# Cosine attention and a Highway layer on one core: the casts of v, the engines of the small operations, and the order of the Highway sum

## The chip, the cores and the metric

The kernel runs on one core of a Trainium2 chip. A core has a matrix engine (PE, with its weight loads as PEld), a vector engine (DVE), a scalar engine (ACT), GpSimd (POOL) and a synchronising engine (SP) that issues most DMAs here. Each engine runs its own instructions in program order; semaphores order them against each other. Matmuls write to PSUM[...]; DVE and ACT read it. The metric is the device time in microseconds of one execution, the median over the runs.

## The reference

Attention over 8 batches of 12 heads, 448 positions, head dimension 64, with q and k normalised, and then a Highway layer over the 3,584 x 768 result:

```python
q_n = q / (norm(q) + 1e-06);  k_n = k / (norm(k) + 1e-06)
attn = softmax(q_n @ k_n.T / tau)          # tau = 0.1
x = (attn @ v)                             # heads side by side: 3584 x 768
H = maximum(x @ w_h, 0.0)
T = 1.0 / (1.0 + exp(-(x @ w_t + b_t)))
out = T * H + (1.0 - T) * x
```

## The kernel before

**Tiling.** The heads are taken four at a time: 24 "quads" Q, three to a batch. A quad is loaded as two tiles raw (q and k, 128 partitions x 14 groups of 64); a batch's v is loaded in three pieces into vr. Each position is p x 7 + c, so a partition holds seven positions of a head.

**Steps of a quad.** `squares` makes sq = raw x raw on the engine that SQ_E names for the quad (ACT in one instruction, POOL in two, lines 369 and 373) and sums it on DVE (line 389); where FOLDS is 1 or 2, POOL first folds the row once or twice (lines 416 and 422). `rsqrt` takes one over the root: on ACT with Ln and Exp for the first seven quads, later on DVE with a shift and two Newton steps over a batch. `norms` multiplies (line 525, the engine from NORM: one instruction on DVE, two on POOL), and qn is turned by PE and a copy or by a DMA transpose on SP (TURN). `cast_v` casts v from 32 to 16 bits into vm (line 583) by the table VM: "A" is ACT, "D" is DVE with both sides read in order, "U" is DVE with the two inner dimensions exchanged on both sides, so that its reads are 64 elements apart. vm has a 65th column of 2.0, so that attention times vm gives the sum of the row too.

**Scores and products.** `quad` makes the scores in seven pieces (line 620, PSUM tiles sp, two of them), ACT takes the exp (line 631), PE multiplies with vm (line 671, tile u), and DVE divides (lines 704, 722, 714). Because of the 2.0, what is kept in x is half of the attention's output.

**The FFN.** 28 tiles n of 128 rows: three for each batch and one more for each two batches (xtail). x is turned by PE with a copy (DVE or ACT) or by DMA (table XT), then four quarters follow: w_t and w_h for the first 384 columns, w_t and w_h for the last. A quarter accumulates 6 matmuls, or 7 where the bias enters as a row of ones, in one of two PSUM tiles pt. In the last six tiles (TAIL) it is the two halves of a score tile sp, and DVE adds the bias (line 836). With t = tanh of the w_t quarter (line 846) and h the w_h quarter, three DVE operations make the sum:

```python
g  = (t - 1) * x           # line 850, tt and x both in SBUF
pt = (t + 1) * h           # line 867, in place in PSUM
o  = max(pt, 0) - g        # line 874
```

**The order.** No loop writes the instructions in the order in which they run. `Plan.run` lists every operation with an engine, a guessed duration, what it depends on and a due time, and simulates: on each engine it takes the ready operation with the smallest start plus LATE times its due time. An operation marked "lock" is taken to exclude POOL while it runs. Where the durations or tables change, the order on all engines, SP's DMA queue among them, changes with them. `P.buf(name, n)` makes the owner of a buffer wait for all users of the one n before it.

Of the kernel before, what the change touches and what calls it, by code (L numbers as in the profile page):

```python
# [8 lines left out]
FP32 = mybir.dt.float32  # L9
FP16 = mybir.dt.float16  # L10
# [10 lines left out]
class Plan:  # L21
# [6 lines left out]
    SLACK = 1.3  # L28
    AHEAD = 15
    NEAR = 60  # L30
    LATE = 0.04

    def __init__(self):
        self.ops = []
# [128 lines left out]
def kernel(  # L163
# [11 lines left out]
    nc = tc.nc  # L175
# [42 lines left out]
    ones_row = const.tile([128, 128], FP16)  # L218
    eps = const.tile([128, 1], FP32)
    NV = 2  # L220
    SQ_E = ("DPPAAAAAAAAAAAAAAPPPPAAP", "PPAPPPPPPPAAAAAAAAPAPPAA")
    FOLDS = "000000000002012200000210"
    NORM = ("DPPPPDPPPPDPPPPPPPDPDDDP", "DDDPPPPPPPPDPPPPPPPPPPPP")
    TURN = ("ADDDSSSSSSSSSSSSSSSSSSSS", "DDDDASSSSSSSSSSSSSSSSSSS")
    XT = "DDDDDDSDSAASSSSSAASSSSSSDAAA"
    ENG = {"A": "ACT", "D": "DVE", "P": "POOL"}
    PAIR = 12
    NEWT = 8
    LATER = 3
    W_AT = 16  # L230
    RS = "AAAAAAADDDDDDDDDDDDDDDDD"
    VM = "UAAAAAUUUUUUUDDDDDDADDAU"
    TAIL = 6
    vm_b = [const.tile([128, 6, C, 66], FP16, name=f"vm{i}") for i in range(NV)]
    e_b = [const.tile([128, 14 * S + 64], FP16, name=f"e{i}") for i in range(2)]
# [170 lines left out]
    def folds(Q, t, sq_ops, level, ring):  # L406

        ringf, waitf = P.buf(f"fold{t}", 2)
        first = []
        for i in range(1):  # L410
            def f(i=i):
                if i == 0:
                    st["fold", Q, t] = fold_p.tile([128, NT, D // 2], FP32, name=f"fold{t}")
                g = slice(0, NT)
                sq = st["sq", Q, t]
                nc.gpsimd.tensor_add(  # L416
                    st["fold", Q, t][:, g, :], sq[:, g, 0 : D // 2], sq[:, g, D // 2 : D]
                )
            first.append(op("POOL", 900, None, sq_ops + ([("first", first)] if first else waitf), f))
        def h():  # L420
            x = st["fold", Q, t]
            nc.gpsimd.tensor_add(
                x[:, :, 0 : D // 4], x[:, :, 0 : D // 4], x[:, :, D // 4 : D // 2]
            )
        last = op("POOL", 520, None, first, h) if level == 2 else first[0]
        ring += first
        ringf += first + [last] * (level == 2)
        st["ring_fold", Q, t] = ringf
        return [last]

    logs = []

    def rsqrt_act(b, qd, reds):

# [13 lines left out]
    def rsqrt(b, qd, n, reds):  # L448
        due = None
        if RS[NQ * b + qd] == "A":  # L450
            return rsqrt_act(b, qd, reds)
        eng = "DVE" if b < NEWT else "POOL"
        lens = (90 if n == 1 else 150, 190 if n == 1 else 290)

        def tiles():
            n2, rs = nrm_tiles(b)
            return n2[:, qd : qd + n, :], rs[:, qd : qd + n, :]

        def f0():
            x, y = tiles()  # L460
            nc.vector.tensor_single_scalar(
                y.bitcast(I32), x.bitcast(I32), 1, ALU.arith_shift_right
            )

        def f1():
            _, y = tiles()
            nc.vector.tensor_scalar(
                out=y.bitcast(I32), in0=y.bitcast(I32), scalar1=-1.0,
                scalar2=float(0x5F3759DF), op0=ALU.mult, op1=ALU.add,
            )  # L470

        ring_ta, wait_ta = P.buf("ta", 2)
        last = op("DVE", lens[0], due, reds + wait_ta, f0, kind="lock")
        last = op("DVE", lens[0], due, [last], f1, kind="lock")
        ta = {}

        def newton(i, it):
            e = nc.vector if eng == "DVE" else nc.gpsimd

            def f():  # L480
                x, y = tiles()
                if i == 0 and it == 0:
                    ta[0] = ta_p.tile([128, NQ, NG], FP32, name="ta")
                a = ta[0][:, 0:n, :]
                if eng == "DVE":
                    if i == 0:
                        e.scalar_tensor_tensor(out=a, in0=y, scalar=-0.5, in1=x, op0=ALU.mult, op1=ALU.mult)
                    elif i == 1:
                        e.tensor_mul(a, a, y)
                    else:  # L490
                        e.scalar_tensor_tensor(out=y, in0=a, scalar=1.5, in1=y, op0=ALU.add, op1=ALU.mult)  # L491
                elif i == 0:
                    e.tensor_mul(a, y, x)
                elif i == 1:
                    e.tensor_mul(a, a, y)
                elif i == 2:
                    e.tensor_scalar(out=a, in0=a, scalar1=-0.5, scalar2=1.5, op0=ALU.mult, op1=ALU.add)
                else:
                    e.tensor_mul(y, a, y)
            return f  # L500

        for it in range(2):
            for i in range(3 if eng == "DVE" else 4):
                last = op(eng, lens[0] if eng == "DVE" else lens[1], due, [last], newton(i, it),
                          kind="lock" if eng == "DVE" else "")
                ring_ta.append(last)
        return last
# [67 lines left out]
    def cast_v(b):  # L575
        ring, wait = P.buf("vm", NV)
        vm = vm_b[b % NV]
        outs = []
        for i in range(NQ):
            def f(i=i):  # L580
                how = VM[NQ * b + i]
                dims = "p i d c" if how == "U" else "p i c d"
                (nc.scalar.copy if how == "A" else nc.vector.tensor_copy)(  # L583
                    vm[:, 2 * i : 2 * i + 2, :, 0:D].rearrange(f"p i c d -> {dims}"),
                    st["vr", b][:, 2 * i : 2 * i + 2, :].rearrange(f"p i (c d) -> {dims}", c=C),
                )
            how = VM[NQ * b + i]
            outs.append(op(
                "ACT" if how == "A" else "DVE", {"A": 840, "D": 540, "U": 990}[how], None,
                wait + [o_fv[b % NV], st["gotv", b][i]], f, kind="lock" if how == "D" else "",  # L590
            ))
        ring += outs
        st["ring_vr", b] += outs
        st["vm", b] = (ring, outs)


# [2 lines left out]
    def quad(Q):  # L599
# [78 lines left out]
        for rnd, when in enumerate((t_step(Q, 6), t_step(Q, 6) + 2.5)):  # L678
# [3 lines left out]
            for i in range((6, 2)[rnd]):  # L682
                def f(i=i, rnd=rnd, key=key):
                    if i == 0:
                        st[key] = u_ps.tile([128, 2, 512], FP32, name="u")
                    t, h = divmod(i, 2)
                    av(st[key], i, h, 384 - 64 * par if rnd else 128 * t)
                a = op("PE", 220, when + 0.01 * i,
                       list(exps.values()) + [o_vm[qd], o_fv[Q % 2]] + ([("first", ops)] if ops else wait_u), f, kind="row")
                ops.append(a)  # L690
            ring_u += ops
            ring_e += ops
# [99 lines left out]
    def quarters(b, t, F, n, loc, c, ringt, ring_x, xf, later):  # L792
        ringo, waito = P.buf("o", N_O)
        fin = []
        for qi, (w_i, mh) in enumerate(((1, 0), (0, 0), (1, 1), (0, 1))):
# [6 lines left out]
            elif w_i == 1:  # L802
                ringq, waitq = P.buf("sp", 2)
            when = F + 1.6 * qi
            groups = ((0, 1, 2), (3, 4, 5)) if w_i == 0 or tail else ((0, 1, 2), (3, 4, 5, 6))
            mms = []
            for gi, grp in enumerate(groups):
                def mm(grp=grp, w_i=w_i, ms=ms, mh=mh, qi=qi, tail=tail):
                    if tail and w_i == 1 and grp[0] == 0:
                        loc["sp", mh] = s_ps.tile([128, 2, 512], FP32, name="sp")  # L810
                    if grp[0] == 0:
                        loc["pt", qi] = (
                            loc["sp", mh][:, 1 - w_i, 0:MH] if tail
                            else p_ps.tile([128, MH], FP32, name="pt", tag="pt")[:, :]
                        )
                    for cc in grp:
                        nc.tensor.matmul(  # L817
                            loc["pt", qi],
                            lhsT=loc["xT"][:, cc, :] if cc < CC else ones_row[:, :],
                            rhs=w_f[w_i][:, cc, ms] if cc < CC else bth[:, ms],  # L820
                            start=(cc == 0), stop=(cc == CC - 1 + (w_i == 1 and not tail)),
                        )
                m = op("PE", 163 * len(grp), when + 0.5 * gi,
                       [c, w_done[w_i][gi]] + w_done[2:] * (len(grp) == 4)
# [6 lines left out]
            if w_i == 1:  # L831
                mms_t = mms
                ready = mms[-1]
                if tail:
                    def fb(qi=qi, ms=ms):
                        nc.vector.scalar_tensor_tensor(  # L836
                            out=loc["pt", qi], in0=b_all[:, ms], scalar=0.5, in1=loc["pt", qi],
# [14 lines left out]
                        in1=xf()[:, ms], op0=ALU.subtract, op1=ALU.mult,  # L852
                    )

                e = op("ACT", 390, None, [ready] + waitg + [("first", [z]) for z in logs], fa)
                carry = op("DVE", 470, None, [e] + waitg, fg, kind="lock")
                ringg += [e, carry]
                ringq.append(e)
                ring_x.append(carry)
                gate = (ringg, e, carry)  # L860
                continue

# [8 lines left out]
            def fo(qi=qi, ms=ms, mh=mh):  # L871
                if mh == 0:
# [2 lines left out]
                    out=loc["o"][:, ms], in0=loc["pt", qi], scalar=0.0, in1=loc["g", mh][:, :],  # L875
                    op0=ALU.max, op1=ALU.subtract,
                )

            e1 = op("DVE", 470, F + 3.5 + 3.2 * mh, [mms[-1], e], fh)
            e2 = op("DVE", 470, F + 4 + 3.2 * mh, [e1, carry] + ([("first", fin[:1])] if fin else waito), fo)  # L880
# [4 lines left out]
        if t < 3:  # L885
            def fd():
                r0 = b * S + 128 * t
                nc.sync.dma_start(out[r0 : r0 + 128, :], loc["o"][:, :])
# [88 lines left out]
```

## Time and profile before

| | |
|---|---|
| median of 13 runs | 300.23 us (296.74 to 302.09) |
| of these, near 297.5 / near 300.5 | 6 / 7 |
| the profiled execution | 297.66 us, its span 295.9 us |
| mean granted PE clock | 0.973 |
| PE, DVE, ACT, POOL busy | 245.7, 248.8, 208.1, 150.4 us |

The span cut into 40 slices of 7.4 us, a digit for the tenths in which each engine is busy:

```profile
PE   0368778799878797989889999999999999887880
...
DVE  4888739699999999999999999999999665686773
ACT  1399899899867797676777789977987678311310
POOL 3989569725769937299539965940480000000000
```

The first two slices fill the pipeline. Loads and the small operations of the quads run up to about 225 us, where POOL ends. The scores of the last quad end at 252 us, and six tiles of the FFN are left after that.

### The profile page before, as it was taken

To read this page: it belongs to the slowest core of one execution; us is meant where nothing else is said; L and a number is where in the kernel's file an instruction comes from. 1 tells how busy PE (TensorE), PEld (TensorE's weight loads), DVE (VectorE), ACT (ScalarE), POOL (GpSimd) and SP (SyncE) were. 2 spreads that over 40 slices of the span, in tenths; PEclk is the share of its full clock that TensorE was granted. 3 is DMA by queue.
4 is the path that set the end of the run, shared out by engine and by line. 5 is a ranking of instruction groups with operands and counts; after the bars stand their busy time and mean duration, and the time that the engine had idled before them with its cause. 6 is when DMAs were issued, how large, how long until landed. Compare 5 with 4: busy or idle time off the path is not lost.

```text
span 295.9 us, 9873 instructions
## 1 busy us (share of the span) xinstructions
PE 245.7 (83%) x4229; PEld 138.5 (47%) x4229; DVE 248.8 (84%) x493; ACT 208.1 (70%) x284; POOL 150.4 (51%) x142
## 2 busy tenths in 40 slices
PE   0368778799878797989889999999999999887880
PEld 0235544354444453535455555455554554554540
DVE  4888739699999999999999999999999665686773
ACT  1399899899867797676777789977987678311310
POOL 3989569725769937299539965940480000000000
PEclk9999799799979999799999999999999999999998
DMA  7999939989997999779998999995399233111122
GB/s 262 375 367 269 253 70 320 223 252 297 355 206 196 247 147 362 206 135 234 300 271 185 287 208 336 199 239 105 86 160 188 83 83 82 55 55 53 55 106 53
DMA packets 72060, 58.94 MB, mean 199 GB/s; under 512 B 48336, under 2 KB 68304, under 8 KB 72016
## 3 DMA queue, kind: packets, MB, share of 16 engines
q1 hardware_dynamic: 70144, 55.49, 74.3%
q0 software_dynamic: 1600, 2.36, 4.4%
q8 instruction: 33, 0.54, 0.8%
q10 hardware_dynamic: 272, 0.46, 0.4%
q14 instruction: 11, 0.09, 0.1%
HBM read 38.14 MB, written 11.01 MB: 166 GB/s over the span
## 4 chain that ended last, share of the span: by engine, by line
PE 39%; DVE 35%; ACT 4%; issue 4%; DMA 1%; POOL 1%; ACTq 0%; DVEq 0%
PE pt L817 19%; PE u L671 8%; PE sp L620 6%; DVE n L389 6%; DVE g L850 5%; DVE vm L583 5%; PE sp L817 4%; DVE o L874 4%; DVE pt L867 3%; DVE x L722 3%; DVE sp L836 2%; ACT tt L846 2%; ACT e L631 2%; DVE qn L525 2%; DMA xT<-xtail 1%
## 5 line engine op out<-in xcount | busy, mean ns | idle before, releaser
L631 ACT ACTIVATE e<-sp 128x896 f16<-128x896 f32 x168 | 145.4, 922 | 29.5 <-PE sp L620 27.7
L525 POOL TENSOR_TENSOR qn<-raw,rs 128x448 f16<-128x448 f32 x74 | 84.1, 1165 | 57.4 <-DVE rs L491 27.9
L817 PE MATMUL pt<-w,xT 128*128 128x384 f16 x528 | 103.3, 331 | 10.3 <-DVE o L874 7.4
L817 PEld LDWEIGHTS <-xT 128*128 128x128 f16 x672 | 59.8, 98 | 66.6 <-issue 26.5
L671 PE MATMUL u<-vm,e 64*128 64x65 f16 x2688 | 58.9, 195 | 5.0 <-DVE x L722 4.3
L671 PEld LDWEIGHTS <-e 64*128 64x128 f16 x2688 | 49.2, 97 | 29.1 <-issue 16.4
L620 PE MATMUL sp<-qT,qT 64*64 64x448 f16 x672 | 55.7, 380 | 6.5 <-ACT e L631 4.8
L389 DVE TENSOR_REDUCE n<-sq 128x7 f32<-128x448 f16 x72 | 41.7, 607 | 3.0 <-POOL sq L369 1.6
L850 DVE SCALAR_TENSOR_TENSOR g<-tt,x 128x384 f16<-128x384 f16 x48 | 34.8, 724 | 8.8 <-ACT tt L846 8.6
L846 ACT ACTIVATE tt<-pt 128x384 f16<-128x384 f32 x44 | 21.9, 497 | 14.1 <-ACT e L631 8.4
L817 PE MATMUL sp<-w,xT 128*128 128x384 f16 x144 | 25.4, 326 | 6.1 <-ACT tt L846 2.9
L867 DVE SCALAR_TENSOR_TENSOR pt<-tt,pt 128x384 f32<-128x384 f16 x44 | 25.1, 570 | 6.4 <-PE pt L817 4.4
L620 PEld LDWEIGHTS <-qT 64*64 64x64 f16 x672 | 15.1, 106 | 31.1 <-issue 25.7
L583 DVE CAST vm<-vr 128x896 f16<-128x896 f32 x17 | 28.2, 1666 | 0.0
L365 ACT ACTIVATE sq<-raw 128x896 f16<-128x896 f32 x28 | 26.2, 963 | 0.0
L874 DVE SCALAR_TENSOR_TENSOR o<-pt,g 128x384 f32<-128x384 f32 x44 | 24.4, 555 | 1.4
L722 DVE TENSOR_TENSOR x<-u,rd 128x384 f16<-128x384 f32 x48 | 24.6, 551 | 0.8
L846 ACT ACTIVATE tt<-sp 128x384 f16<-128x384 f32 x12 | 5.9, 490 | 25.3 <-DVE sp L836 15.6
L369 POOL TENSOR_TENSOR sq<-raw 128x448 f16<-128x448 f32 x19 | 20.7, 1088 | 4.2 <-DMA raw<-in_k_dram 4.2
L373 POOL TENSOR_TENSOR sq<-raw 128x448 f16<-128x448 f32 x19 | 20.0, 1052 | 0.0
L416 POOL TENSOR_TENSOR fold<-sq 128x448 f32<-128x448 f16 x12 | 14.4, 1206 | 7.5 <-ACT sq L365 7.5
L704 DVE RECIPROCAL rd<-u 128x12 f32<-128x12 f32 (+1 forms) x48 | 9.8, 205 | 9.3 <-PE u L671 8.8
(46 smaller groups left out, 157.8 us busy)
## 6 DMA issues: line engine op xcount, KB each, us to landing
raw<-in_q_dram SPq DMA_DIRECT2D x24, 448.0 KB, 6.1
vr<-in_v_dram SPq DMA_DIRECT2D x24, 448.0 KB, 6.5
raw<-in_k_dram SPq DMA_DIRECT2D x23, 448.0 KB, 6.1
out_dram<-o SPq DMA_DIRECT2D x24, 384.0 KB, 3.9
out_dram<-o SPq DMA_DIRECT2D x8, 192.0 KB, 2.7
w<-in_moe_w_t_dram POOLq DMA_DIRECT2D x2, 576.0 KB, 11.5
w<-in_moe_w_h_dram POOLq DMA_DIRECT2D x2, 576.0 KB, 12.6
qT<-qn SPq DMA_TRANSPOSE x39, 5.0
```

Of the source, the lines that this page charges most:

```text
L389: nc.vector.reduce_sum(n2[:, qd, NT * t + g0 : NT * t + g0 + n], src()[:, g0 : g0 + n, 0:width], axis=AX.X,)
L525: (nc.vector if eng == "DVE" else nc.gpsimd).tensor_mul(st["qn", Q, t][:, :, :].rearrange("p c (h d) -> p h c d", h=2)[:, h0:h1, c0:c1, :] ...
L583: (nc.scalar.copy if how == "A" else nc.vector.tensor_copy)(vm[:, 2 * i : 2 * i + 2, :, 0:D].rearrange(f"p i c d -> {dims}"), st["vr", b][ ...
L620: nc.tensor.matmul(sp[64 * half : 64 * half + 64, h, 0:S].rearrange("x (c p) -> x c p", c=C), lhsT=kT[hp, ci, 64 * half : 64 * half + 64], ...
L631: nc.scalar.activation(e[:, o : o + 2 * S].rearrange("x (a p c) -> x a p c", a=2, c=C), st["sp", Q, ci][:, :, 0:S].rearrange("x a (c p) -> ...
L671: nc.tensor.matmul(u[:, s, slot * (D + 1) : (slot + 1) * (D + 1)], lhsT=e[sp, o : o + 128], rhs=vm[sp, 2 * qd + h, c, 0 : D + 1], start=(c ...
L722: nc.vector.tensor_mul(st["x", b][:, :, 4 * qd : 4 * qd + 4, :].rearrange("p t (h s) d -> p t h s d", s=2)[:, :, :, s, :], u[:, s, :, 0:D] ...
L817: nc.tensor.matmul(loc["pt", qi], lhsT=loc["xT"][:, cc, :] if cc < CC else ones_row[:, :], rhs=w_f[w_i][:, cc, ms] if cc < CC else bth[:, ms],
L846: nc.scalar.activation(loc["tt", mh][:, :], loc["pt", qi], AF.Tanh)
L850: nc.vector.scalar_tensor_tensor(out=loc["g", mh][:, :], in0=loc["tt", mh][:, :], scalar=1.0, in1=xf()[:, ms], op0=ALU.subtract, op1=ALU.mult,
L867: nc.vector.scalar_tensor_tensor(out=h, in0=loc["tt", mh][:, :], scalar=1.0, in1=h, op0=ALU.add, op1=ALU.mult)
L874: nc.vector.scalar_tensor_tensor(out=loc["o"][:, ms], in0=loc["pt", qi], scalar=0.0, in1=loc["g", mh][:, :], op0=ALU.max, op1=ALU.subtract,)
```

## The change

The casts of v marked "U" become two casts of one head each, read in order; the table VM is new. In tiles marked "R" (all but four) the Highway sum is 2x + (1+t)(relu(h) - x), in which each step has one operand in PSUM. In the four tiles marked "P" g is made on POOL, in two operations. SQ_E, FOLDS, NORM and one or two places of XT have other engines, the planner's LATE is 0.025 instead of 0.04, some guessed durations change, and the load of the tanh table is an operation of its own with a due time.

```diff
-    LATE = 0.04
+    LATE = 0.025
...
-    SQ_E = ("DPPAAAAAAAAAAAAAAPPPPAAP", "PPAPPPPPPPAAAAAAAAPAPPAA")
-    FOLDS = "000000000002012200000210"
-    NORM = ("DPPPPDPPPPDPPPPPPPDPDDDP", "DDDPPPPPPPPDPPPPPPPPPPPP")
+    SQ_E = ("DPAAAAAAPAAAAAPAADPAAAAP", "PPAPPPPPPAAPAAAAAAPPPPPP")
+    FOLDS = "000000000002012110000110"
+    NORM = ("DDDPPDPPPPPPPPPPPPPPDPPP", "DPPPPPPPPPPPPPPPPPPPPDPP")
...
-    XT = "DDDDDDSDSAASSSSSAASSSSSSDAAA"
+    XT = "DDDDDDSDSAASSSSSSDSSSSSSDAAA"
...
-    NEWT = 8
+    GATE = "RRRRRRRRRRRRRRRRRRRRPPPPRRRR"
+    BIAS = "MMMMMMMMMMMMMMMMMMMMMMDDDDDD"
...
-    VM = "UAAAAAUUUUUUUDDDDDDADDAU"
+    SW_AT = 48
+    VM = "AAAAAAUDUDDDDDDDUDDDAAAA"
...
-                dims = "p i d c" if how == "U" else "p i c d"
-                (nc.scalar.copy if how == "A" else nc.vector.tensor_copy)(
-                    vm[:, 2 * i : 2 * i + 2, :, 0:D].rearrange(f"p i c d -> {dims}"),
-                    st["vr", b][:, 2 * i : 2 * i + 2, :].rearrange(f"p i (c d) -> {dims}", c=C),
-                )
...
+            for h0, n in ((0, 1), (1, 1)) if how == "U" else ((0, 2),):
+                def f(g=slice(2 * i + h0, 2 * i + h0 + n), how=how):
+                    (nc.scalar.copy if how == "A" else nc.vector.tensor_copy)(
+                        vm[:, g, :, 0:D],
+                        st["vr", b][:, g, :].rearrange("p i (c d) -> p i c d", c=C),
+                    )
...
+                def fg1(ms=ms, mh=mh):
+                    loc["g", mh] = ff_p.tile([128, MH], FP16, name="g")
+                    nc.gpsimd.tensor_mul(loc["g", mh][:, :], loc["tt", mh][:, :], xf()[:, ms])
+
+                def fg2(ms=ms, mh=mh):
+                    g = loc["g", mh][:, :]
+                    nc.gpsimd.tensor_sub(g, g, xf()[:, ms])
+
+                if not switch:
+                    def fs():
+                        nc.scalar.preload_act_table(AF.Tanh)
+
+                    switch.append(op("ACT", 1300, SW_AT, [("first", [z]) for z in logs], fs))
...
+            if not carry:
+                def fd(qi=qi, ms=ms):
+                    h = loc["pt", qi]
+                    nc.vector.scalar_tensor_tensor(
+                        out=h, in0=h, scalar=0.0, in1=xf()[:, ms], op0=ALU.max, op1=ALU.subtract
+                    )
+
+                def fr(qi=qi, ms=ms, mh=mh):
+                    if mh == 0:
+                        loc["o"] = out_p.tile([128, DM], FP32, name="o")
+                    nc.vector.scalar_tensor_tensor(
+                        out=loc["o"][:, ms], in0=xf()[:, ms], scalar=2.0, in1=loc["pt", qi],
+                        op0=ALU.mult, op1=ALU.add,
+                    )
+
+                e0 = op("DVE", 470, F + 3.2 + 3.2 * mh, [mms[-1]], fd)
+                e1 = op("DVE", 470, F + 3.5 + 3.2 * mh, [e0, e], fh)
+                e2 = op("DVE", 470, F + 4 + 3.2 * mh, [e1] + ([("first", fin[:1])] if fin else waito), fr)
```

fh, the step (t+1) x what stands in pt, is the same in both forms; the form before stays for the four tiles marked "P". BIAS names the tiles that TAIL named before.

## The prediction

> **What bounds the kernel.** I first read the span cut into stages, because the shares of the whole (PE 83%, DVE 84%, ACT 70%) mix stages with different limits. Columns: length of the stretch, busy us and instructions of PE, PE's weight loads, DVE, ACT and POOL, then the granted clock.
>
> ```profile
> 15.00:19.20 4.20, 2.39 (x20) 0.54 (x16) 4.20 (x7) 4.20 (x8) 3.14 (x2) 1.00 1.06 388
> 19.20:60.00 40.80, 32.02 (x653) 19.95 (x653) 28.06 (x56) 37.62 (x54) 32.96 (x35) 0.92 0.99 238
> 60.00:220.00 160.00, 146.38 (x2636) 80.80 (x2635) 154.43 (x310) 128.83 (x171) 103.60 (x94) 0.98 0.97 229
> 220.00:253.00 33.00, 32.69 (x608) 18.10 (x600) 23.42 (x45) 24.55 (x33) 0.48 (x1) 1.00 0.49 104
> 253.00:296.00 43.00, 29.40 (x318) 17.41 (x310) 28.73 (x59) 9.02 (x17) 0.00 (x0) 0.97 0.18 65
> ```
>
> From 19 to 60 us ACT is nearly full (37.6 of 40.8). From 60 to 220 us DVE is full (154.4 of 160) while PE has 13.6 us of holes. From 220 to 253 us PE has none (32.7 of 33). The end is a relay between engines.
>
> Next I asked who holds PE up (the waits: waiter, releaser, us in all, times, longest) and what DVE spends its time on (the groups).
>
> ```profile
> ACT tt L846 <- DVE sp L836: 15.6, 8, 2.8
> ...
> PE pt L817 <- DVE o L874: 7.4, 7, 2.2
> ...
> PE u L671 <- DVE x L722: 4.3, 6, 1.5
> ```
>
> ```profile
> L850 DVE SCALAR_TENSOR_TENSOR g<-tt,x 128x384 f16<-128x384 f16 x48 | 34.8, 724 | 8.8 <-ACT tt L846 8.6
> L583 DVE CAST vm<-vr 128x896 f16<-128x896 f32 x17 | 28.2, 1666 | 0.0
> L874 DVE SCALAR_TENSOR_TENSOR o<-pt,g 128x384 f32<-128x384 f32 x44 | 24.4, 555 | 1.4
> L525 DVE TENSOR_TENSOR qn<-raw,rs 128x896 f16<-128x896 f32 x11 | 14.9, 1362 | 0.1
> L836 DVE SCALAR_TENSOR_TENSOR sp<-b_all,sp 128x384 f32<-128x384 f32 x12 | 6.7, 558 | 2.6 <-PE sp L817 2.5
> ```
>
> Inside 60 to 220 us the waits of PE on DVE's o and x, summed stretch by stretch, are 12.4 of the 13.6 us. The groups show two swollen rows: g takes 724 ns though its neighbour o, of the same 384 elements, takes 555; and the casts of v average 1,666 ns.
>
> **1. The casts of v.** The 17 DVE casts are two kinds. One at a time in the timeline, the 9 strided ones take 2.16 to 3.08 us, 21.9 in all; the 8 contiguous ones 0.61 to 1.31, 6.3 in all (mean 0.79). After: 10 quads on ACT (7 before), 11 contiguous casts on DVE, and 3 quads as two casts of one head. The half cast is in no row: between 0.31 (half of 0.61) and 0.61 (448 elements at the pace of the reduction, 607 ns); I take 0.45. DVE then pays 11 x 0.79 + 6 x 0.45 = 11.4, for 28.2 before. Inside 60 to 220 us it is 22.7 before (13 casts) and 11 x 0.87 (the mean of the 6 contiguous ones there) + 2.7 = 12.3 after: **-10.4**.
>
> Do the contiguous casts then fight with POOL? The Trainium skill (SBUF — State Buffer, Who interferes with whom) says that a cast in a two-port mode and a GpSimd instruction take the shared port pair whole, and whoever comes second is blocked to the end. That speaks against contiguous casts: 11 of them, each behind one POOL operation of 0.93 us, would add 10.2 us and eat the gain. The row of the contiguous casts says 0.87 against 0.61 undisturbed, 2.9 us for 11, already in my sum. And the strided form is no way out, as the timeline shows:
>
> ```profile
> 96.56 2.25 DVE L583 CAST vm<-vr 128x896 f16<-128x896 f32 x1
> 96.72 2.87 POOL L416 TENSOR_TENSOR fold<-sq 128x448 f32<-128x448 f16 x1
> ```
>
> That fold takes 1.03 us elsewhere; it stood behind the strided cast. I take the row.
>
> **2. The Highway sum.** In 24 of 28 tiles g = (t-1)x (two SBUF operands) goes, and relu(h)-x comes, with one operand in PSUM; the other two steps keep the shape of fh and fo (570 and 555 ns). The new step is closest to the bias row L836 (one PSUM operand, written back to PSUM): 558 ns. So 724 becomes 558. The rule against it: the table of perf modes in VectorE: DVE Perf Modes (The perf-mode tier table) gives a 16-bit tensor_tensor in SBUF twice the rate of one with any PSUM operand. By that g would lose 384/2/0.96 GHz = 0.20 us per operation in moving to PSUM, 48 x 0.20 = 9.6 us lost (an estimate from that page). The trace disagrees for this operation: undisturbed, g takes 0.54 to 0.56 us from 16-bit SBUF operands, what o takes from PSUM. I follow the trace. In 60 to 220 us g is 27.44 us for 35 (784 each): 35 x 0.558 = 19.5, **-7.9**.
>
> The other 4 tiles (20 to 23, 8 halves) keep g, but as two POOL operations each, about 0.8 us apiece (384/448 of POOL's 0.93), at a time when POOL is empty (0.5 us after 220).
>
> **3. Engines chosen anew.** DVE's normalisations go from 11 to 7; in 60 to 220 us from 6 (8.57 us) to 2 (2.9): **-5.7**. Squares +1 (1.09) and xT copies +1 (0.55): **+1.6**. Reductions go from 72 at 607, 8 at 377 and 4 at 608 to 68, 4 and 10: 49.1 against 48.9, nothing. POOL gets 8 normalisations (1,165 each), 2 squares, 2 first folds more and 4 second folds fewer: about +10 on 103.6 of 160 us, still under 75%. ACT: 3 casts more, 2 squares and 2 copies fewer, +0.9 in all over stages where it has 20% to spare, except the first (below). One more xT transposition on SP's queue, 1 on 13.
>
> Sum for DVE in 60 to 220 us: -10.4 - 7.9 - 5.7 + 1.6 = -22.4. Its load falls from 154.4 to 132 of 160 us: **DVE stops being the bound there, PE is next** (146.4). So the gain is not 22 us. It is what PE's holes hold: at most 12.4, at least 0. A queue at 83% still makes others wait, so I take two thirds, **-8**.
>
> **4. What the new order moves.** The planner's weight and tables shift everything, so I counted PE's instruction order. At the end of the seventh quad's scores 3.6 tiles of the FFN are done instead of 2.8; at the end of the last, 22.4 in both. A tile is some 25.5 matmuls of 163 ns (2.22 us for 13 less 1.08 for 6, in the chain), 4.2 us: 0.8 tile, 3.3 us, moves into the stage to 60 us, where PE has 8.8 us of holes, out of a later one that has few. Less 0.8 us of tanh on ACT, full there: between 0 and -3.3, I take **-2**. Changes between kinds of matmul rise from 278 to 294; 16 at the 0.0 to 0.3 us that a weight load waits at such a change: **+1**.
>
> Start: ACT now has a cast (0.93) and a square (0.95) ahead of the first qT copy, which ended at 12.58 us; DVE's copy, at 14.03, set the first scores. ACT's other work behind it is the exps. Between 0 and +1.9, and the cast waits for v's load (6.8 us at the earliest after its issue at 2.3, 16.8 for the slowest of four): I take **+0.7**.
>
> **5. A PSUM bank is held longer.** Of the two pt banks, that of h is now released after three DVE operations instead of two: with 0.1 us at each end 1.9 us instead of 1.35. Cover is the PE work up to the next user of the bank. By the new order and the trace's marginal times its median is 2.3 us; over the 40 halves that use pt in the new form, what lies under 1.9 adds up to 2.3 us. **+2**. Queued behind the relu step in DVE's order are the other steps, x and the reductions; PE waits for x.
>
> **6. The tail.** Tiles 24 to 27: the new step runs while tanh does (DVE stands still there, "g <- ACT tt" 5.3 us), so fh can follow tanh at once: about 0.5 us per tile, -2. Tiles 22 and 23 hold a score bank for two POOL operations in place of g: 1.6 + 0.3 of handing over - 0.56 = 1.3 per half, partly beside PE's other bank: +1.5. Together **-0.5**.
>
> At nothing: the explicit table load (one load in either kernel), the BIAS table (the same tiles as the tail had), the removed POOL form of the square root (not used).
>
> **Sum:** -8 - 2 + 1 + 0.7 + 2 - 0.5 = -6.8; 6 transposes fewer on PE -0.5; and PE's runs, cut up less by waits, save pipeline fills of 0.2 us at about 13 of them, -2.5. Forecast **-9.8**: 297.66 us of the profiled execution (span 295.9 and 1.8 around it) become 287.9. That execution is one of 6 near 297.5; the other 7 of the 13 lie near 300.5 and the median, 300.23, among them. Half of that offset of 2.6 on top gives **289.5**.
>
> **Rivals.** (a) PE takes the bound over at once: the holes are filled by waits on ACT (128.8 of 160, and "e <- PE sp" 27.7 us shows how ACT and PE hand over), and only a third of the 12.4 comes back (4.1 in place of 8) and the 2.5 of the fills does not: 6.4 less gained, 296 (294 to 301). For: PE at 98% with DVE at 71% in 220 to 253 us. Against: DVE's waits are named. (b) It goes better: with strided casts gone POOL's blocked operations shrink too, and all of the 12.4 and of the 3.3 comes back: 5.7 more, 283.8 (279 to 284). (c) **Slower:** the bank of part 5. If one other DVE operation (a reduction, 0.61) stands in front of each of the three steps' first, the hold is 2.5 us, and over the same 40 halves the missing cover is 13.3 us instead of 2.3: with the relief of (a), 289.5 + 11 + 6.4 = 307. It decides from about 2.3 us of hold. For: DVE's order is fixed and its steps have fixed places. Against: at 83% the queue is rarely that long. (d) That the change doesn't act is excluded by the instruction counts.
>
> **Numbers.** Forecast 0.54 (284 to 294), (a) 0.20, of which 0.06 within 0.5% of 300.23 (what a measurement here can tell from no change), (b) 0.13, (c) 0.13. Faster 0.81, same 0.06, slower 0.13. The range 281 to 298 leaves out (c) and the upper end of (a).
>
> **Signs.** DVE near 132/160 of its stage and PE above 93%; the new relu step near 560 ns and no cast above 1.4 us; "pt <- DVE o" below 3 us. Wrong if DVE's load falls as said and PE's holes stay, or if PE's waits for the last step of the sum grow.

## The result, and the profile after

The changed kernel takes **287.98 us** (median of 11 runs, 287.35 to 289.19). All runs of the kernel before, those made beside the experiments included, have a median of 299.11 us (48 runs, 296.73 to 302.09). The ratio is 0.965, with a 95% interval of 0.962 to 0.968. The forecast was 289.5. The profiled execution took 289.13 us, with a span of 287.4, 8.5 us shorter than the span of before.

To see where the 8.5 us came from, the span is best cut at an event, not at a time: the start of the last exp, where the attention ends and the last FFN tiles begin. First before (columns as in the prediction: the stretch, its length, busy us and instructions of PE, weight loads, DVE, ACT, POOL, then the clock, the DMA share and GB/s):

```profile
0.00:60.00 60.00, 37.19 (x691) 22.18 (x692) 42.16 (x81) 45.68 (x66) 46.30 (x50) 0.94 0.97 269
60.00:253.00 193.00, 179.06 (x3232) 98.90 (x3229) 177.85 (x354) 153.38 (x203) 104.08 (x94) 0.98 0.88 207
253.00:295.90 42.90, 29.40 (x318) 17.41 (x310) 28.73 (x59) 9.02 (x17) 0.00 (x0) 0.97 0.18 65
```

And the same view of after, with two stretches more that the text uses:

```profile
0.00:60.00 60.00, 42.24 (x737) 24.42 (x737) 44.53 (x86) 49.78 (x72) 41.24 (x47) 0.97 0.98 277
...
19.20:60.00 40.80, 36.87 (x699) 21.92 (x696) 30.93 (x60) 39.91 (x58) 29.47 (x33) 0.96 1.00 249
60.00:210.00 150.00, 141.14 (x2652) 78.80 (x2652) 138.71 (x308) 123.97 (x164) 99.40 (x104) 1.00 1.04 246
...
60.00:240.10 180.10, 171.07 (x3183) 95.06 (x3183) 154.81 (x341) 148.09 (x197) 106.68 (x112) 1.00 0.93 220
240.10:287.40 47.30, 30.04 (x312) 17.52 (x308) 27.84 (x55) 8.92 (x17) 7.28 (x8) 0.96 0.17 59
```

The attention ends 12.9 us earlier (240.1 against 253.0) and the tail is **4.4 us longer** (47.3 against 42.9). Taking PE's busy time from each length gives its holes:

| PE | before | after | difference |
|---|---|---|---|
| holes to 60 us | 22.8 | 17.8 | -5.0 |
| holes from 60 us to the last exp | 13.9 | 9.0 | -4.9 |
| holes in the tail | 13.5 | 17.3 | +3.8 |
| busy, whole span | 245.7 | 243.4 | -2.3 |

The sum is the span's -8.5, but for rounding. The groups show the new DVE work (busy us, mean ns, then the idle time before it and what ended it):

```profile
L821 PE MATMUL pt<-w,xT 128*128 128x384 f16 x528 | 102.4, 327 | 1.1 <-DVE o L915 0.6
...
L908 DVE SCALAR_TENSOR_TENSOR pt<-pt,x 128x384 f32<-128x384 f32 x36 | 20.2, 560 | 8.1 <-PE pt L821 7.8
...
L915 DVE SCALAR_TENSOR_TENSOR o<-x,pt 128x384 f32<-128x384 f16 x36 | 19.9, 552 | 1.0
...
L586 DVE CAST vm<-vr 128x896 f16<-128x896 f32 x11 | 10.7, 985 | 0.0
...
L586 DVE CAST vm<-vr 128x448 f16<-128x448 f32 x6 | 3.4, 610 | 0.0
```

The new relu step takes 560 ns where g took 724, and the DVE casts take 14.1 us where they took 28.2. The waits of after (waiter, releaser, us in all, times, longest):

```profile
ACT tt L850 <- PE sp L821: 25.9, 10, 3.6
...
PE sp L821 <- DVE sp L840: 8.9, 10, 1.4
DVE sp L908 <- ACT tt L850: 8.5, 8, 1.3
DVE pt L908 <- PE pt L821: 7.8, 9, 1.6
...
PE u L674 <- DVE x L725: 5.7, 7, 1.4
...
PE pt L821 <- DVE o L915: 0.6, 3, 0.2
```

"pt <- DVE o", 7.4 us before, has all but gone. A line that before did not show in this size stands near the top: PE waits 8.9 us for the bias step (L840, a tile sp, so the tail).

### The profile page after: what moved, and what is told of

It is laid out like the page before. It is cut to its first block, busy times and chain, and to the rows that moved or that the text cites. A ratio compares the mean times of both kernels' runs of the same rounds, so it can differ in the third digit from the quotient of the medians.

```text
span 287.4 us, 9911 instructions
## 1 busy us (share of the span) xinstructions
PE 243.4 (85%) x4223; PEld 137.0 (48%) x4223; DVE 227.2 (79%) x481; ACT 206.8 (72%) x283; POOL 155.2 (54%) x166
## 4 chain that ended last, share of the span: by engine, by line
DVE 39%; PE 38%; ACT 10%; issue 4%; POOL 4%; DMA 2%; DVEq 0%; ACTq 0%
PE pt L821 16%; PE u L674 9%; PE sp L623 7%; ACT e L634 6%; DVE n L391 5%; PE sp L821 5%; DVE o L915 5%; DVE pt L893 4%; DVE x L725 4%; DVE pt L908 4%; DVE qn L527 3%; DVE vm L586 2%; DVE sp L840 2%; ACT tt L850 2%; DMA raw<-in_k_dram 2%
## 5 line engine op out<-in xcount | busy, mean ns | idle before, releaser
L527 POOL TENSOR_TENSOR qn<-raw,rs 128x448 f16<-128x448 f32 x82 | 81.0, 1018 | 42.2 <-DVE rs L493 33.7
L821 PE MATMUL pt<-w,xT 128*128 128x384 f16 x528 | 102.4, 327 | 1.1 <-DVE o L915 0.6
L821 PEld LDWEIGHTS <-xT 128*128 128x128 f16 x672 | 58.9, 97 | 60.4 <-issue 26.3
L674 PEld LDWEIGHTS <-e 64*128 64x128 f16 x2688 | 48.4, 96 | 32.2 <-issue 18.0
L391 DVE TENSOR_REDUCE n<-sq 128x7 f32<-128x448 f16 x68 | 39.1, 609 | 1.0 <-ACT sq L367 0.3
L821 PE MATMUL sp<-w,xT 128*128 128x384 f16 x144 | 26.2, 325 | 10.0 <-DVE sp L840 8.9
L371 POOL TENSOR_TENSOR sq<-raw 128x448 f16<-128x448 f32 x20 | 20.0, 1002 | 17.2 <-DMA raw<-in_k_dram 8.7
L908 DVE SCALAR_TENSOR_TENSOR pt<-pt,x 128x384 f32<-128x384 f32 x36 | 20.2, 560 | 8.1 <-PE pt L821 7.8
L367 ACT ACTIVATE sq<-raw 128x896 f16<-128x896 f32 x26 | 24.3, 962 | 1.7 <-DVE n L391 0.7
L915 DVE SCALAR_TENSOR_TENSOR o<-x,pt 128x384 f32<-128x384 f16 x36 | 19.9, 552 | 1.0
L375 POOL TENSOR_TENSOR sq<-raw 128x448 f16<-128x448 f32 x20 | 19.8, 991 | 0.0
L418 POOL TENSOR_TENSOR fold<-sq 128x448 f32<-128x448 f16 x14 | 14.7, 1062 | 4.7 <-ACT sq L367 4.7
L551 PE MATMUL tp<-ident,qn 128*128 128x128 f16 x63 | 6.7, 270 | 11.7 <-DVE qn L527 11.5
```

What stands on the lines that cost most here:

```text
L367: nc.scalar.activation(o, i, AF.Square)
L391: nc.vector.reduce_sum(n2[:, qd, NT * t + g0 : NT * t + g0 + n], src()[:, g0 : g0 + n, 0:width], axis=AX.X,)
L527: (nc.vector if eng == "DVE" else nc.gpsimd).tensor_mul(st["qn", Q, t][:, :, :].rearrange("p c (h d) -> p h c d", h=2)[:, h0:h1, c0:c1, :] ...
L674: nc.tensor.matmul(u[:, s, slot * (D + 1) : (slot + 1) * (D + 1)], lhsT=e[sp, o : o + 128], rhs=vm[sp, 2 * qd + h, c, 0 : D + 1], start=(c ...
L821: nc.tensor.matmul(loc["pt", qi], lhsT=loc["xT"][:, cc, :] if cc < CC else ones_row[:, :], rhs=w_f[w_i][:, cc, ms] if cc < CC else bth[:, ms],
L908: nc.vector.scalar_tensor_tensor(out=h, in0=h, scalar=0.0, in1=xf()[:, ms], op0=ALU.max, op1=ALU.subtract)
```

## The experiments

Two questions are open. Which of the parts brought the 12.9 us? And why does the tail cost 4.4 us, where the prediction had it half a us shorter? All ratios are to the kernel before, measured beside the kernel in question, with a 95% interval.

**1. The casts alone.** The kernel before, with the strided casts read in order and nothing else changed. The order of instructions on every engine stays as it was.

```diff
-                dims = "p i d c" if how == "U" else "p i c d"
+                dims = "p i c d"
```

> The kernel before with nothing changed but the access pattern of the nine strided casts: one cast of two heads, read in order. The order of instructions on every engine stays that of before. Theory (DVE's service time fills PE's holes between 60 and 220 us, and a strided cast blocks POOL as well): DVE's busy time falls by 9 x (2.43 - 0.85) = 14 us, PE's idle time in the stage by about half of what the whole change took (some 2 to 3 us), and the time by 3 to 6 us, to 292-295. Rival (a relieved engine alone returns little while the order stays that of before; the new order brings the gain): DVE falls by the same 14 us and the time by less than 1.5 us.

Measured: 287.34 us (287.19 to 287.51, 4 runs), ratio 0.960 (0.953 to 0.967). That is the time of the whole change (the two intervals overlap). The casts gave 11.2 us (298.58 to 287.34), where the theory expected 3 to 6 and the rival less than 1.5. The stages of this kernel, cut at its last exp:

```profile
60.00:242.80 182.80, 177.40 (x3241) 98.30 (x3238) 165.76 (x355) 153.71 (x205) 99.56 (x95) 1.00 0.94 220
242.80:285.60 42.80, 29.35 (x314) 17.39 (x308) 28.77 (x59) 8.96 (x17) 0.00 (x0) 0.96 0.18 65
```

Its waits from 60 to 242.8 us:

```profile
PE pt L817 <- DVE o L874: 1.7, 4, 0.6
...
PE u L671 <- DVE x L722: 0.8, 2, 0.4
```

In the same stretch of before the two are 7.4 and 3.4 us. PE's holes after 60 us fall from 13.9 to 5.4 and its busy time by 1.7: 10.2 us together, from 12.1 us less DVE work there. The tail is the old one. So the casts are enough by themselves. (The 1.7 of busy time needn't be fewer pipeline fills: the granted clock of the stage is 1.00 here and 0.98 in before, and the two weren't told apart.) DVE's share of the stage hardly moved (92% before, 91% here). A share of 92% therefore said little about how late DVE was for PE.

**2. Everything but the casts.** The changed kernel with the old cast function and its table.

```diff
-    VM = "AAAAAAUDUDDDDDDDUDDDAAAA"
+    VM = "UAAAAAUUUUUUUDDDDDDADDAU"
...
+                dims = "p i d c" if how == "U" else "p i c d"
...
+                    vm[:, 2 * i : 2 * i + 2, :, 0:D].rearrange(f"p i c d -> {dims}"),
```

> The changed kernel with the casts of v as before: nine strided ones and the table VM of before; sum, engines and order as changed. Theory (the casts are what fills PE's holes; the rest of DVE's relief comes on top of a stage where PE has become the bound): +8 to +12 us, 296 to 300, DVE busy near 240 us, and PE's idle time in the middle as before. Rival (either relief of DVE alone fills the holes, so 13 us less from sum and normalisations do as well as the casts): 289 to 292.

Measured: 303.02 us (301.73 to 304.29), ratio 1.014 (1.006 to 1.022): slower than before. The attention ends at 253.9 us, as in before, and the tail is 47.2. The theory expected 296 to 300. DVE has less to do than in before, and this helps nothing:

```profile
60.00:253.90 193.90, 175.17 (x3206) 97.68 (x3204) 168.56 (x344) 149.35 (x199) 120.30 (x112) 0.98 0.88 211
```

DVE is at 87% of the stage, and PE has 18.7 us of holes, more than the 13.9 of before at 92%. What fills the place is POOL: 120.3 us, where the changed kernel has 106.7. The timeline shows the costliest spot (start, us, engine, operation, idle time before it and its releaser):

```profile
104.70 7.38 POOL L527 TENSOR_TENSOR qn<-raw,rs 128x448 f16<-128x448 f32 x4
...
106.37 5.01 DVE L585 CAST vm<-vr 128x896 f16<-128x896 f32 x2
...
112.04 3.96 POOL L418 TENSOR_TENSOR fold<-sq 128x448 f32<-128x448 f16 x2
...
113.01 2.23 DVE L585 CAST vm<-vr 128x896 f16<-128x896 f32 x1
...
119.46 1.02 DVE L724 TENSOR_TENSOR x<-u,rd 128x384 f16<-128x384 f32 x2
...
120.53 0.67 PE L673 MATMUL u<-vm,e 64*128 64x65 f16 x18 [5.12 <-DVE x L724]
```

Three strided casts hold DVE for 7.2 us and hold POOL's operations beside them as well: four qn take 7.38 us where four at the 1,018 ns of the changed kernel would take 4.1, and two folds 3.96 where two at 1.03 would take 2.1. DVE's reductions behind them wait for POOL's folds, x comes late, and PE stands for 5.1 us. A strided cast delays two engines, one behind the other. The order differs from that of after, because the planner was told other durations. Experiment 5 will show that a new order alone can cost some 6 us, so the 15 us to the changed kernel need not all be the casts' doing.

**3. Half casts in the place of the strided ones.** The kernel before; each strided cast becomes two contiguous ones of a head each, as in the change, and the order stays.

```diff
-                dims = "p i d c" if how == "U" else "p i c d"
...
+                for g in (slice(2 * i, 2 * i + 1), slice(2 * i + 1, 2 * i + 2)) if how == "U" else (slice(2 * i, 2 * i + 2),):
```

> The kernel before with each of the nine strided casts as two casts of one head, in order; the plan stays that of before. In the changed kernel such a half cast took 0.61 us, as long as a whole contiguous one, and none was longer where POOL ran, so two of them cost DVE 1.22 us and POOL nothing. Theory (DVE's time decides): DVE falls by 9 x (2.43 - 1.22) = 11 us, the time by 11/14 of the 11.2 us of the whole casts, to about 289.5. Rival (POOL's freedom decides, since strided casts block it): as fast as the whole casts or faster, 286.5 to 287.5.

Measured: 286.91 us (286.19 to 287.52), ratio 0.960 (0.952 to 0.967): where the rival saw it, not the theory, and the time of experiment 1. The group of the half casts in this kernel:

```profile
L583 DVE CAST vm<-vr 128x448 f16<-128x448 f32 x18 | 10.2, 608 | 0.0
```

And the second fold on POOL here, with its shortest, median and longest duration:

```profile
L422 POOL TENSOR_TENSOR fold<-fold x8: 656/661/859, 83.7 to 165.0; 128x224 f32<-128x224 f32 x8
```

A pair costs DVE 1.22 us where the whole cast costs 0.84 on average (experiment 1), so DVE pays some 3 us more. In return POOL is left alone: that fold's longest is 0.86 us here, 1.79 in experiment 1 and 2.35 in before. The total is the same, and DVE's busy time is not longer either (234.3 us, 235.0 in experiment 1). Whether these two effects cancel, or whether neither counts once the strided form is gone, this run can't tell.

**4. The casts, with the planner told of them.** The kernel before with "D" for every "U" in VM, so that the order is made for contiguous casts.

```diff
-    VM = "UAAAAAUUUUUUUDDDDDDADDAU"
+    VM = "DAAAAADDDDDDDDDDDDDADDAD"
```

> The kernel before with the nine strided casts marked as contiguous in the table, so that the planner knows their duration (540 ns instead of 990) and that they exclude POOL; the same instructions as in the run that only changed the access pattern, in an order planned anew. Theory (the instructions decide, the order is second): 287.3 within 1.5 us. Rival (every new plan shifts the time by several us either way, as the run with only the planner's weight changed suggests): 284 or below, or 290 or above.

Measured: 287.45 us (286.03 to 289.97), ratio 0.962 (0.953 to 0.971), as the theory had it. The new order brings nothing that could be measured over the old one, and costs nothing.

**5. The sum, the engines and the order, each undone.** Three kernels, each the changed one with one part put back: the old sum in all tiles, the old tables of engines, and the planner's old weight. The last changes no operation at all, only the order.

```diff
-    GATE = "RRRRRRRRRRRRRRRRRRRRPPPPRRRR"
+    GATE = "DDDDDDDDDDDDDDDDDDDDDDDDDDDD"
```

> The changed kernel with the old Highway sum on DVE in all 28 tiles (g from two SBUF operands), also in the four tiles that POOL served. Theory: g costs 0.78 us against 0.56 where POOL is busy, 35 x 0.22 = 8 us more for DVE in the middle stage, which is at 139 of 150 us: +3 to +4 us, 291-292. Rival (the new form is what made the tail 4.4 us longer, from the end of the last exp to the end of the span): the middle loses 3 and the tail wins 3 to 4 back, no difference that can be told.

```diff
-    SQ_E = ("DPAAAAAAPAAAAAPAADPAAAAP", "PPAPPPPPPAAPAAAAAAPPPPPP")
-    FOLDS = "000000000002012110000110"
-    NORM = ("DDDPPDPPPPPPPPPPPPPPDPPP", "DPPPPPPPPPPPPPPPPPPPPDPP")
+    SQ_E = ("DPPAAAAAAAAAAAAAAPPPPAAP", "PPAPPPPPPPAAAAAAAAPAPPAA")
+    FOLDS = "000000000002012200000210"
+    NORM = ("DPPPPDPPPPDPPPPPPPDPDDDP", "DDDPPPPPPPPDPPPPPPPPPPPP")
...
-    XT = "DDDDDDSDSAASSSSSSDSSSSSSDAAA"
+    XT = "DDDDDDSDSAASSSSSAASSSSSSDAAA"
```

> The changed kernel with the engine tables of before for squares, folds, normalisations and xT. Theory: DVE gets 4 normalisations back (5.7 us, 2 of them at the end of the stage), POOL loses 8: +1.5 to +3 us, 289.5 to 291. Rival (the tables decide which work is early, and the FFN that is pulled ahead of 60 us comes from them): the first stage loses its 4.9 us of filled PE holes and the time rises by 4 us or more.

```diff
-    LATE = 0.025
+    LATE = 0.04
```

> The changed kernel with the planner's LATE back at 0.04, everything else as changed. Theory: the tables and forms carry the gain and the weight only shuffles: within 1 us of 288.0. Rival (the weight pulls the FFN ahead, 0.8 tile more by 60 us, which filled 4.9 us of PE's holes there): +3 to +5 us, and PE's idle time between 19 and 60 us near 8.8 us again.

| put back | us | ratio (interval) | DVE busy, whole span | last exp at |
|---|---|---|---|---|
| nothing (the change) | 287.98 | 0.965 (0.962 to 0.968) | 227.2 | 240.1 |
| the sum | 293.69 | 0.979 (0.969 to 0.988) | 233.9 | 246.6 |
| the tables | 294.23 | 0.984 (0.975 to 0.992) | 232.7 | 245.5 |
| LATE | 294.32 | 0.986 (0.976 to 0.995) | 228.9 | 245.1 |

Each loses about 6 us, and so does the one with no operation changed. The three theories had expected 3 to 4, 1.5 to 3 and less than 1; in the second and the third case the rival, that what moves early is lost, came nearer (4 or more, 3 to 5), but PE's holes from 19.2 to 60 us, 3.9 in the changed kernel, grow only to 5.8 and 6.3. Three times 6 is more than the whole gain, so these are not shares of it: an order that falls otherwise can alone cost that much (in experiment 4 a new order cost nothing). What the sum and the tables are worth apart from the order stays open. What can be said is what all the rest of the change does together, the new order included: it takes the attention's end from 242.8 us (experiment 1) to 240.1, 2.7 us for some 7 us less DVE work up to there (DVE's busy time less its tail: 206.2 and 199.4).

**6. The tail.** The four last tiles repeat a pattern. Its timeline in the changed kernel:

```profile
270.66 2.11 PE L821 MATMUL sp<-w,xT 128*128 128x384 f16 x12 [1.09 <-DVE sp L840]
...
271.39 0.49 ACT L850 ACTIVATE tt<-sp 128x384 f16<-128x384 f32 x1 [2.35 <-PE sp L821]
271.91 0.56 DVE L908 SCALAR_TENSOR_TENSOR sp<-sp,x 128x384 f32<-128x384 f32 x1 [1.31 <-ACT tt L850]
272.51 0.56 DVE L893 SCALAR_TENSOR_TENSOR sp<-tt,sp 128x384 f32<-128x384 f16 x1
272.98 0.56 DVE L840 SCALAR_TENSOR_TENSOR sp<-b_all,sp 128x384 f32<-128x384 f32 x1
...
273.59 2.17 PE L821 MATMUL sp<-w,xT 128*128 128x384 f16 x12 [0.83 <-DVE sp L840]
```

PE waits for the bias step before every 12 matmuls. In the new order the bias step is written between the two groups of three in which w_h's six matmuls are planned. It adds to the w_t half of the tile sp, they write the w_h half; but it is one tile, and so the second group carries a wait for DVE. In before this happens in the first half of the tail only; from 273.6 us on all 24 matmuls of two halves run through, and the bias step comes beside them, behind both groups:

```profile
PE sp L817 <- DVE sp L836: 2.1, 3, 0.7
...
279.05 4.06 PE L817 MATMUL sp<-w,xT 128*128 128x384 f16 x24 [0.87 <-ACT tt L846]
...
281.20 0.56 DVE L836 SCALAR_TENSOR_TENSOR sp<-b_all,sp 128x384 f32<-128x384 f32 x1 [0.52 <-PE sp L817]
```

The first line is the wait that is 8.9 us in the changed kernel. A tile takes 6.47 us there (one after another from 257.72, 264.19, 270.66 to 277.13) and 5.44 in before (273.61 to 279.05); four times the difference is 4.1 of the 4.4 us. Theory: that position of the bias step. Two rivals: the new sum, of which three DVE steps now follow tanh on the same tile; and the POOL operations of tiles 20 to 23. The first kernel plans w_h's six matmuls as one operation in the last six tiles, so that nothing can come between them; else the order is that of the change, on PE, DVE, ACT and POOL alike, as the traces show.

```diff
             groups = ((0, 1, 2), (3, 4, 5, 6)) if w_i == 1 and by_mm else ((0, 1, 2), (3, 4, 5))
+            if tail and w_i == 0:
+                groups = ((0, 1, 2, 3, 4, 5),)
...
-                       [c, w_done[w_i][gi]] + w_done[2:] * (len(grp) == 4)
+                       [c] + w_done[w_i][gi : gi + 1 + (len(grp) == 6)] + w_done[2:] * (len(grp) == 4)
```

> The changed kernel with one edit in the last six tiles: the six matmuls of a w_h quarter are one operation of the plan and no longer two of three. In the changed kernel DVE's bias step is written between the two groups, and since both write the same PSUM tile sp (different halves) the second group waits for it; in the kernel before the bias step came behind both groups. Theory (that wait is what made the tail 4.4 us longer): the tail falls from 47.3 to 43-44 us, the time to 284-285. Rival (the third DVE step behind the matmuls makes the tail longer): within 1 us of 288.0.

Measured: **284.29 us** (283.85 to 286.06), ratio 0.953 (0.944 to 0.962). The tail falls from 47.3 to 43.5 us, a tile to 5.56; the 3.8 us of the tail are the 3.7 of the medians (287.98 and 284.29). (The two profiled spans differ by 1.9 us more, ahead of the tail: with the same order the last exp starts at 240.1 us in the changed kernel and at 238.2 here. A difference of some 2 us between two profiles there is scatter.) Its timeline:

```profile
264.52 4.06 PE L823 MATMUL sp<-w,xT 128*128 128x384 f16 x24 [1.16 <-ACT tt L852]
264.53 0.57 DVE L910 SCALAR_TENSOR_TENSOR sp<-sp,x 128x384 f32<-128x384 f32 x1 [0.16 <-ACT tt L852]
...
266.67 0.56 DVE L842 SCALAR_TENSOR_TENSOR sp<-b_all,sp 128x384 f32<-128x384 f32 x1 [0.38 <-PE sp L823]
...
270.08 4.06 PE L823 MATMUL sp<-w,xT 128*128 128x384 f16 x24 [1.50 <-ACT tt L852]
```

PE now runs 24 matmuls in one go, the bias step beside them. Nothing else was moved, so the position of the bias step is what cost it. The rivals one by one: the old sum in the last four tiles alone (this also plans the last tiles anew),

```diff
-    GATE = "RRRRRRRRRRRRRRRRRRRRPPPPRRRR"
+    GATE = "RRRRRRRRRRRRRRRRRRRRPPPPDDDD"
```

> The changed kernel with the old sum on DVE in the last four tiles. The bias step still stands between the two groups of w_h. Theory (the wait between the groups): no gain, 287 to 289. Rival (the new form's extra step behind the matmuls): the tail falls by 3 to 4 us, to 284-285.

gave 285.96 us (284.71 to 286.59), ratio 0.956 (0.949 to 0.964), and a tail of 44.9, between what theory and rival expected. The wait for the bias step is still there ("PE sp L821 <- DVE sp L840" 6.1 us, up to 0.7 a time in place of 1.4). So 2.4 of the 4.4 us go with the sum as well: by the timelines, the stall's length depends on how many DVE steps stand ahead of the bias step and how closely they follow each other. In the new form the step after L908 starts 0.60 us behind it, whose result it needs; in the old form it starts 0.48 behind g. Both edits shorten the same wait, and 3.8 and 2.4 are more than the 4.4; the two together were not tried. And the kernel of one group without the POOL gates,

```diff
-    GATE = "RRRRRRRRRRRRRRRRRRRRPPPPRRRR"
+    GATE = "RRRRRRRRRRRRRRRRRRRRRRRRRRRR"
```

> The changed kernel with the w_h quarter as one operation in the last six tiles and the new sum in all 28 tiles, none on POOL. Theory (two POOL operations in place of one DVE step hold the score banks of tiles 22 and 23 longer by some 0.3 to 1.3 us per half): the tail falls by 0.5 to 2 us against 43.5, the time to 282.5-284. Rival (POOL takes work from DVE where DVE is the relay's slow side): the tail grows by 1 to 2 us, 285 to 286.

gave 286.13 us (285.68 to 286.23), ratio 0.956 (0.948 to 0.965), with a tail of 43.5, as with them: the POOL gates cost the tail nothing, and neither theory nor rival had its tail right. What it is slower by lies in the attention phase, which is in another order and ends at 241.0 instead of 238.2.

**7. The bias as a row of ones in the tail too.** If the bias step is in the way, PE can add the bias by a seventh matmul. First by the table, which makes the planner plan anew:

```diff
-    BIAS = "MMMMMMMMMMMMMMMMMMMMMMDDDDDD"
+    BIAS = "MMMMMMMMMMMMMMMMMMMMMMMMMMMM"
```

> The changed kernel with the w_h quarter as one operation in the last six tiles, and the bias of those tiles as a seventh matmul (the row of ones) in place of DVE's bias step. Theory (the tail is a relay in which PE waits for DVE's steps): 12 steps of 0.56 us leave DVE, 12 matmuls of 0.16 us come to a PE that stands still a third of the tail; a tile's period falls from 5.56 to about 5 us, the tail from 43.5 to 40-41, the time to 281-282. Rival (each half's tanh has to wait for all 13 matmuls of its half anyway, so that the period stays): 284 to 285.

Measured: 287.52 us (286.41 to 288.29), ratio 0.961 (0.954 to 0.969). The tail is 40.4 us, as the theory had it and 3.1 shorter than with one group alone, but the attention ends at 244.2, 6 us later. Most of that loss lies from 84 to 128 us. Some of its waits there:

```profile
POOL fold L418 <- ACT sq L367: 8.0, 2, 5.7
DVE pt L910 <- PE pt L823: 7.9, 4, 6.1
...
ACT sq L367 <- POOL fold L418: 5.1, 1, 5.1
PE sp L623 <- ACT e L634: 4.8, 1, 4.8
```

ACT waits for POOL, POOL for ACT, and PE for ACT, in a stretch that the edit doesn't touch. So the second attempt keeps the plan: the operation of the bias step stays in it and emits nothing, and the second group of w_t emits the seventh matmul.

```diff
-                    for cc in grp:
+                    for cc in grp + (6,) * (tail and w_i == 1 and grp[0] == 3):
...
-                            start=(cc == 0), stop=(cc == CC - 1 + (w_i == 1 and by_mm)),
+                            start=(cc == 0), stop=(cc == CC - 1 + (w_i == 1)),
...
                     def fb(qi=qi, ms=ms):
-                        nc.vector.scalar_tensor_tensor(
...
+                        pass
```

> The kernel with the w_h quarter as one operation in the last six tiles, and in its unchanged plan the twelve bias steps of DVE there write nothing while each w_t quarter gets a seventh matmul with the row of ones: the order of everything else stays that of the run with one group. Theory (the bias row shortens the tail's relay by 3 us, and the 6 us that the newly planned bias row lost ahead of it came from its order alone): last exp at 238 us as with one group, tail 40-41 us, 281 to 282.5 us. Rival (the row of ones delays the attention phase itself): last exp near 244 us, 286 to 288.

Measured: **280.60 us** (279.67 to 281.05, 6 runs), ratio 0.938 (0.932 to 0.943). It beats both kernels, as the theory had it. The attention ends at 239.3 us and the tail is 39.5. A tile of the tail takes 4.78 us:

```profile
258.21 1.14 PE L823 MATMUL sp<-w,xT 128*128 128x384 f16 x6
...
259.18 0.33 PE L823 MATMUL sp<-bth,ones_row 128*128 128x384 f16 x1
...
259.34 2.11 PE L823 MATMUL sp<-w,xT 128*128 128x384 f16 x12
...
260.56 0.49 ACT L849 ACTIVATE tt<-sp 128x384 f16<-128x384 f32 x1 [1.49 <-issue]
...
262.98 1.14 PE L823 MATMUL sp<-w,xT 128*128 128x384 f16 x6
```

The row holds PE for 0.16 us (it starts at 259.18, the next matmul at 259.34), and tanh no longer waits for a DVE step. The kernels of this experiment differ in the order of the attention phase, not in its work, so the 5 us between their last exps (244.2 and 239.3) come of the order, but for the scatter of some 2 us.

## Why the prediction was right, and where it was not

The forecast was -9.8 on the profiled execution, and 289.5 for the median, with half of the offset between the two groups of runs of before added. The span fell by 8.5 us and the median came to 287.98. The mechanism held: DVE kept PE waiting, less DVE work fills PE's holes, and the gain is far less than the DVE work saved. The sizes of its terms held in their sum and not one by one:

- **DVE's sum** (-22.4 from 60 to 220 us) was near in size: from 60 us to the last exp DVE does 23.0 us less, of which 2.4 moved ahead of 60 us; over the whole span it is 21.6. The normalisations of part 3 fell from 8.6 to 2.9 us there, as said. What was drawn from it was half right. PE did go above 93% (94% from 60 to 210 us), but DVE did not fall to 132 of 160: it is at 138.7 of 150, 92%. The same work passes in a shorter time, and its end lies earlier.
- **Two thirds of 12.4 us, -8, with -2 for work moved early.** In the changed kernel PE's holes fell by 4.9 us from 60 us on and by 5.0 before: right as a sum, 9.9 for 10, and by luck, for neither term has its size.
- **What the casts were worth** is mis-sized too: they were 10.4 of the 22.4, so by proportion they would have brought not quite half of the -8. In experiment 1 they alone took 8.5 us of holes, with 12.1 us less DVE work, and PE's busy time fell by 1.7, where -2.5 stood for fewer pipeline fills. Why these microseconds count for more than the others stays open: the first relief may fill most of the holes, or it counts that a strided cast holds POOL as well. Experiment 2, in which DVE did 9.3 us less than in before and PE's holes grew, speaks for the second, but in an order of its own.
- **Part 1, the price of the casts.** 14.1 us against 11.4. A half cast takes 0.61, not 0.45: the upper bound given was the value. The whole ones average 0.985 us, not 0.79, the longest 1.36 (that of before is 1.36 too, not 1.31). That contiguous casts and POOL block each other is visible in that row, but it costs 4.0 us there (10.7 less 11 at 0.61), not the 10.2 of one POOL operation each; and strided casts hold POOL too, as the spot in experiment 2 shows.
- **Part 2.** 560 ns for the step, 558 forecast. The old g ran from 0.54 to 1.40 us, the new one from 0.547 to 0.567: with one operand in PSUM it no longer swells. The Trainium skill (SBUF — State Buffer, Who interferes with whom) says that a DVE instruction with two SBUF inputs contends with POOL's reads and one with a single SBUF input, outside the two-port modes, doesn't; these two ranges agree. The row of the perf-mode table that the prediction weighed is one for tensor_tensor, and these steps are scalar_tensor_tensor; the trace was rightly put first.
- **Part 4.** -2 expected of work moved before 60 us; PE's holes from 19.2 to 60 us fell by 4.9 (8.8 to 3.9). Experiment 1, in the old order, has 9.4 there, so this gain comes with the new tables and order, not with the casts; with the old LATE it is 6.3. (Experiment 6 has 5.2 with the same order up to there, so a microsecond is scatter.) The start cost 0 instead of 0.7: the first qT copy on ACT begins at 11.64 us, in before at 11.67, since v had landed and the cast was done early.
- **Part 5, the bank, +2**, did not come: "pt <- DVE o" fell to 0.6 us. Rival (c) falls with it. Rival (a), that PE takes over at once, did not happen either; of rival (b), POOL's relief is real (experiment 2), but not all holes closed.
- **Part 6, the tail, -0.5, is the step that failed**: +4.4. The prediction let the new step run "while tanh does". In the tail it does not: all eight of them wait for tanh ("sp L908 <- ACT tt", 8.5 us), while those on a tile of their own wait for PE only ("pt L908 <- PE pt"). That the shared tile sp makes them wait is read from the trace and was not tried. And it did not look at where the new order puts the bias step, which experiment 6 shows to be the cost. POOL's g took 0.91 us per operation instead of 0.8; from the last exp to the first matmul of tile 24 it is 0.7 us more (15.4 and 14.7), where +1.5 was said.

In all, the attention gained 12.9 us where the steps gave 9.3, and the tail gave a third of it back. That the forecast came so near is luck: it had two errors of opposite sign.

## What to carry to other kernels

Look for single instructions that are slow and also hold another engine, replace them first, alone, and measure before the rest: here nine casts gave as much as the whole change, while DVE's busy share of its stage hardly moved. In a kernel with a planned order a change of a cost or table can move the time by several us, so an edit is only measured cleanly with the plan kept fixed (an operation that stays in the plan and emits nothing does this). Look at what shares a buffer tile: in this kernel a matmul group waited for a DVE step on the other half of its tile, which cost 3.7 us.

## What the runs showed of the hardware

- A contiguous cast of half the elements is no faster. 128x448 takes 0.608 us (18 of them in experiment 3), the shortest of 128x896 also 0.608 (experiment 1): half the pace. It isn't lengthened by POOL either (0.601 to 0.620 us for all 18), while the whole cast reaches 1.36 us in the changed kernel and 1.48 in experiment 1.
- A cast with reads 64 elements apart takes 2.16 us at its fastest (before), 3.5 times the contiguous one, and holds POOL too: a fold of 1.03 us took 2.87 beside it.
- In a step of three operands, two 16-bit inputs in SBUF are hardly faster than one of them with a 32-bit one in PSUM: 0.540 us at the shortest for 384 elements (g, before) against 0.547 (the new step, after).
